# Weight loads tied to TensorE progress, one queue for the first inputs, and another block order in a fused attention and MLP layer

## The chip, the cores and the metric

The kernel runs on one core of a Trainium2 chip. The metric is the device time of one launch in microseconds, and lower is better. A core has five engines: TensorE (PE in the profile; its weight loads are listed apart as PEld), VectorE (DVE), ScalarE (ACT), GpSimd (POOL) and SyncE (SP). Transfers run on 16 DMA engines, and are issued by instructions on SP's or ACT's queue.

## The reference

One sequence of 2048 tokens of width 448 passes through an attention block and an MLP block, all in bfloat16:

```python
def _A_ref(x, wqkv, wo):               # 16 heads of 28, W, dil = 8, 2
    q, k, v = split(x @ wqkv)
    # token s attends to the tokens s, s-2, ..., s-14; those before the start are masked
    attn = softmax(einsum(q, k[idx]) * 28 ** -0.5)
    return einsum(attn, v[idx]) @ wo

def _B_ref(x, w1, w2, w3, w4):         # w1, w2: 448x448, w3: 448x1792, w4: 1792x448
    h = gelu(layernorm(x) @ w1)
    # the four quarters of h's columns are shifted by +1, -1, +2, -2 tokens
    x1 = x + shifted(h) @ w2
    return x1 + gelu(layernorm(x1) @ w3) @ w4

h = x + _A_ref(layernorm(x), wqkv, wo)
out = h + _B_ref(layernorm(h), w1, w2, w3, w4)
```

## The kernel before, in words

Tokens are handled in eight tiles m of 256 tokens each as they are loaded (two tokens to a partition). Even and odd tokens stand apart, and HT holds the transposed layer norm of 1024 even and 1024 odd tokens. A phase is a function that describes one piece of work on one tile: `phase_LN1(m)` (layer norm of the input and its transpose into HT), `phase_QK(u)` in four parts c (queries and keys), `phase_V(t)` (values), `phase_att(g)` in parts (scores, exp, sums, reciprocal by Ln and Exp, weighted values), `phase_WO(m)` and `phase_LN2(m)`, `phase_W1`, `phase_W2(m)`, `phase_LN3(m)`, `phase_W3(u)` and `phase_W4(u)` with the output's store. The layer norm runs on VectorE and GpSimd; the transposes of the first two tiles run on TensorE and the other 22 (over all three layer norms) as DMA transposes that SP issues.

Attention is made of small matmuls. A part of `phase_att` issues two groups of 64 score matmuls of 57 columns, 8 matmuls for the sums and 64 matmuls of 57 columns for the weighted values, each with its own weight load. The projections issue groups of 28 or more matmuls of 128 to 448 columns.

Nothing of the order on the engines is written by hand. The phases only make a list of operations with durations and dependencies. The planner, `_Sched.schedule` (lines 218 to 352), walks a simulated time: on each engine it takes the ready operation that can begin first, and among those that can begin within SLACK (100 ns) the one whose block stands first in the list `rank` at the end of `_fast_path`. 36 matmuls on zeros, the block "warm", have a late rank and fill TensorE where nothing else is ready. An operation waits by semaphore for each of its `deps`; its `odeps` only order it in the plan and give no wait on the chip.

The loads, with the names used below: `load_x(m)` loads two of the sixteen row groups of the input (xin). `wload` loads a 448-row weight in four pieces (two large, two small), or in eight with `each`. wqk (the query and key weights; its staging tile is called h in the profile, because it borrows the memory of h3) is needed before the first QK phase: `wqk_copies` copies it into the tile arena, which the QK matmuls read. wv are the value weights. `loads_w` (wo, w1, w2), `loads_c` (w3) and `loads_d` (w4) are the later weights, marked `bulk`. In the planner's time a bulk load is not issued before the queue's modelled end less LEAD; on the chip it waits for nothing, and in the plan it stands behind the sixth DMA transpose (`after=trs[5:6]`, an order and not a wait). In the profile w1 to w4 are all called w_s.

All instructions are issued by one helper line in `_plan` (L1324), so the profile's groups are told apart by their tiles.

Of the kernel before, what the change touches and what calls it, by code (L numbers as in the profile page):

```python
# [86 lines left out]
class _Sched:  # L87
# [86 lines left out]
    MODE = 90.0  # L174
    SLACK = 100.0
    SWITCH = 300.0
    LEAD = 500.0
    WINDOW = 3413.0

    def prepare(self):  # L180
        n = len(self.ops)
# [18 lines left out]
    def gated(self, ham, st, work):  # L200

        W = self.WINDOW
        t = st
        while work > 0.0:
            while (ham[0] + 1) * W <= t:
                ham[2] = ham[1] >= 0.38 * W if ham[2] else ham[1] >= 0.9 * W
                ham[0] += 1
                ham[1] = 0.0
            rate = 1.0 if ham[2] else 0.5
            step = min(work / rate, (ham[0] + 1) * W - t)  # L210
            t += step
            ham[1] += step
            work -= step * rate
            if work < 1e-6:
                break
        return t - st

    def schedule(self):
        if not hasattr(self, "children"):
# [53 lines left out]
        mode = None  # L273
        qfree = 0.0
        ham = [0, 0.0, False]
        done = 0
        while done < n:
            best = None
            for e in engs:
                cand = None  # L280
                for op in ready[e]:
                    st = max(arr[op.idx][e], free[e])
                    if op.bulk:
                        st = max(st, qfree - self.LEAD)
                    if cand is not None and st > cand[0] + self.SLACK:
                        continue
                    if op.opts and any(max(t2, free[e2]) + op.opts[e2][1] < st + op.opts[e][1] for e2, t2 in arr[op.idx].items()):
                        continue
                    if op.groups and e == "pe":
                        taken = ()  # L290
                        for g in op.groups:
                            if g not in gbank:
                                at = place(g.n, st, taken)
                                if at is None:
                                    break
                                st = max(st, at[1])
                                taken += tuple(range(at[0], at[0] + g.n))
                        else:
                            at = True
                        if at is None:  # L300
                            continue
                    if e == "act" and op.table is not None and op.table != table:
                        st = max(st, free[e] + self.TABLE) + self.SWITCH
                    if cand is None or st < cand[0] - self.SLACK or (st < cand[0] + self.SLACK and op.prio < cand[1].prio):
                        cand = (st, op)
                if cand is not None and (best is None or cand[0] < best[0]):
                    best = cand + (e,)
            if best is None:
                raise RuntimeError("no op can go: %r" % [(e, [(o.tag, o.idx) for o in ready[e]]) for e in engs])
            st, op, e = best  # L310
            for e2 in (op.opts or (op.eng,)):
                ready[e2].remove(op)
            i = op.idx
            eng_of[i] = e
            dur = op.opts[e][1] if op.opts else op.dur
            if e == "act" and op.table is not None:
                if op.table != table:
                    st -= self.SWITCH
                table = op.table
            if e == "pe":  # L320
                if op.mode != mode:
                    dur += self.MODE
                mode = op.mode
                dur = self.gated(ham, st, dur)
            op.t0 = beg[i] = st
            for g in op.groups:
                if g not in gbank:
                    b = place(g.n, st)[0]
                    gbank[g] = b
                    gleft[g] = len(g.ops)  # L330
                    g.bank = b
                    g.wait = set()
                    g.opener = op
                    for x in range(b, b + g.n):
                        g.wait |= {o for o in held_by[x] if o.eng != "pe"}
                        holder[x] = g
                        held_by[x] = []
                gleft[g] -= 1
                for x in range(gbank[g], gbank[g] + g.n):
                    held_by[x].append(op)  # L340
                    if gleft[g] == 0:
                        holder[x] = None
            if op.is_dma:
                free[e] = st + dur
                qfree = max(st + op.lat[0], qfree) + op.lat[1]
                op.t1 = qfree + op.lat[2]
            else:
                free[e] = st + dur + self.OCC[e]
                op.t1 = st + dur + self.LAT[e]
            fin[i] = op.t1  # L350
            order[e].append(op)
            self.gorder.append(op)
            done += 1
            for ch in self.children[i]:
                npend[ch.idx] -= 1
                if npend[ch.idx] == 0:
                    push(ch)
# [4 lines left out]
    def settle(self):  # L362
        for op in self.ops:
            if op.opts:
                op.eng = self.eng_of[op.idx]
                op.ins = op.opts[op.eng][0]
            for g in op.groups:
                if g.opener is op:
                    op.deps |= g.wait
        for op in self.ops:  # L370
            op.ins = [(m, {k: (v.fn(v.group.bank) if isinstance(v, _PV) else v) for k, v in kw.items()})
                      for m, kw in op.ins]
            for d in op.deps:
                d.users += 1
# [38 lines left out]
def _fast_path(nc, es, flag, A_x, A_wqkv, A_wo, B_w1, B_w2, B_w3, B_w4, out):  # L413
# [63 lines left out]
    def copy(out_ap, in_ap, n):  # L477
# [2 lines left out]
            "act": ([("activation", dict(ka, func=ACT.Copy))], 170 + n / 1.2),  # L480
            "dve": ([("tensor_copy", ka)], (150 + n) / 0.96)}, **ka)

    def dma(chan, out_ap, in_ap, nbytes, dur=450.0, rate=200.0, q="sp", after=(), bulk=False):
        return S.macro(q, [("dma_start", dict(out=out_ap, in_=in_ap))], dur, chan=chan, lat=(1000.0, nbytes / rate, 1150.0),
                       after=after, bulk=bulk)

    def tile(n=1):
        g = _Group(n)
# [16 lines left out]
    def wload(chan, dst, src, qs, after=(), bulk=False, each=False):  # L505
        n = src.shape[1]
        for o in range(2):
            rows = src[64 * o:64 * o + 384, :].rearrange("(i p) n -> p i n", p=128)
            for i in range(3 if each else 1):
                i0, i1 = (i, i + 1) if each else (0, 3)  # L510
                dma(chan + qs[o], dst[:, 2 * i0 + o:2 * i1 + o - 1:2, :], rows[:, i0:i1, :], 128 * n * 2 * (i1 - i0), 600,
                    rate=333.0, q=qs[o], after=after, bulk=bulk)
        for a in range(2):
            dma(chan + qs[a], dst[half[a], 6, :], src[384:448, :] if a == 0 else src[0:64, :], 64 * n * 2, 500, rate=200.0, q=qs[a],
                after=after, bulk=bulk)
# [11 lines left out]
    def setup():  # L527
        S.tag = "setup"
        load_x(0)
        load_x(1, "act")  # L530
        wload("wqk", wst, A_wqkv[:, 0:2 * D], ("sp", "act"))
        load_x(2)
        load_x(3)
        pool("memset", 150, ap=ident[:], constant=0.0)
# [51 lines left out]
    def loads_w():  # L586
        S.tag = "loads_w"
        wov = A_wo.rearrange("(c j d) n -> j d c n", c=4, j=4)
        for j in range(4):
            dma("wo%d" % j, wo_s[32 * j:32 * j + 28, :, :], wov[j], D * D * 2 // 4, 600, rate=150.0, after=trs[5:6], bulk=True)  # L590
        wload("w1", w1_s[:, 0:KB * D].rearrange("p (b n) -> p b n", b=KB), B_w1, ("sp", "sp"), after=trs[5:6], bulk=True)
        dma("w2", w2_s[:], B_w2.rearrange("(c k) n -> k c n", k=112), D * D * 2, 620, rate=300.0, after=trs[5:6], bulk=True)

    def loads_c():
        S.tag = "loads_c"
        wload("w3", w3_s, B_w3, ("sp", "sp"), after=trs[5:6], bulk=True, each=True)

    def loads_d():
        S.tag = "loads_d"
        for f in range(2):  # L600
            dma("w4_%d" % f, w4_s[:, 7 * f:7 * f + 7, :], B_w4[896 * f:896 * f + 896, :].rearrange("(f k) n -> k f n", k=128), D * F,
                740, rate=333.0, after=trs[5:6], bulk=True)

    stc = [0]

# [241 lines left out]
    def w2_ln3(*ms):  # L847
# [55 lines left out]
    phase_W3(3)  # L903
    phase_W4(3)
    rank = {b: k for k, b in enumerate((
# [6 lines left out]
    ).split())}  # L912
    for op in S.ops:
        op.prio = 10000 * rank[op.tag] + op.idx
# [483 lines left out]
```

## Time and profile before

| what | value |
|---|---|
| times of three runs | 214.65, 214.72, 215.84 us; median 214.72 us |
| the profiled execution | 214.2 us, of which its span is 212.5 us |
| TensorE busy | 191.6 us, 90% of the span, 3391 matmuls and as many weight loads |
| VectorE, ScalarE, GpSimd busy | 111.5, 100.4, 48.3 us |
| DMA | 18.13 MB, mean 85 GB/s; the first quarter of the span holds most of it |
| first QK matmul, last matmul of the MLP | 12.22 us, 206.8 us |

The page has a strip of 40 slices of the span, in which each digit is a busy share in tenths. The chain of waits follows the work that ended last backwards: a stretch called "issue" is time in which the engine waited for nothing that the profile shows. A view by windows gives each engine's busy time and number of instructions in a stretch.

### The profile page before, as it was taken

To read this page: it belongs to the slowest core of one execution; us is meant where nothing else is said; L and a number is where in the kernel's file an instruction comes from. 1 tells how busy PE (TensorE), PEld (TensorE's weight loads), DVE (VectorE), ACT (ScalarE), POOL (GpSimd) and SP (SyncE) were. 2 spreads that over 40 slices of the span, in tenths; PEclk is the share of its full clock that TensorE was granted. 3 is DMA by queue.
4 is the path that set the end of the run, shared out by engine and by line. 5 is a ranking of instruction groups with operands and counts; after the bars stand their busy time and mean duration, and the time that the engine had idled before them with its cause. 6 is when DMAs were issued, how large, how long until landed. Compare 5 with 4: busy or idle time off the path is not lost.

```text
span 212.5 us, 7395 instructions
## 1 busy us (share of the span) xinstructions
PE 191.6 (90%) x3391; PEld 129.2 (61%) x3391; DVE 111.5 (52%) x259; ACT 100.4 (47%) x107; POOL 48.3 (23%) x90
## 2 busy tenths in 40 slices
PE   7899998438899989889999999999999999999990
PEld 2367754216667678554977555888555888855540
DVE  5699635403449870989997796100998000012220
ACT  2196696506766898790965100576000566610000
POOL 6333200000003420009435049000079400000000
PEclk9999999856999999999999999999999999999999
DMA  6994799994000430004064105500015500001111
GB/s 221 321 271 88 110 202 278 283 412 112 6 5 0 93 46 3 3 6 88 3 91 58 32 4 129 86 3 3 0 26 117 119 3 3 3 0 43 43 43 54
DMA packets 29532, 18.13 MB, mean 85 GB/s; under 512 B 21112, under 2 KB 28600, under 8 KB 29496
## 3 DMA queue, kind: packets, MB, share of 16 engines
q1 hardware_dynamic: 28872, 16.58, 32.9%
q10 hardware_dynamic: 624, 1.03, 1.5%
q8 instruction: 27, 0.44, 0.8%
q14 instruction: 9, 0.07, 0.1%
HBM read 10.67 MB, written 1.84 MB: 59 GB/s over the span
## 4 chain that ended last, share of the span: by engine, by line
PE 77%; issue 6%; DMA 6%; DVE 5%; POOL 2%; ACT 2%; ACTq 0%
PE ps L1324 77%; DMA h<-in_A_wqkv_dram 4%; DVE xin L1324 2%; DMA HT<-ln 2%; POOL rstd L1324 1%; DVE QK L1324 1%; ACT lnz L1324 1%; DVE ln L1324 1%; DVE xb L1324 0%; DVE st L1324 0%; ACTq L1324 0%; ACT arena L1324 0%; ACT HT L1324 0%; POOL vtmp L1324 0%; DVE pt L1324 0%
## 5 line engine op out<-in xcount | busy, mean ns | idle before, releaser
L1324 PE MATMUL ps<-HT,w_s 64*128 64x256 bf16 (+1 forms) x1064 | 56.3, 264 | 0.8 <-DMA HT<-ln 0.6
L1324 PEld LDWEIGHTS ps<-HT,w_s 64*128 64x128 bf16 x1064 | 49.9, 94 | 7.1 <-DMA HT<-ln 0.9
L1324 DVE TENSOR_TENSOR xb<-ps,xb 128x448 bf16<-128x448 f32 (+1 forms) x24 | 18.4, 772 | 54.2 <-PE ps L1324 54.1
L1324 ACT ACTIVATE QK<-ps 128x1024 bf16<-128x1024 f32 (+2 forms) x24 | 22.7, 951 | 25.9 <-PE ps L1324 25.8
L1324 POOL TENSOR_SCALAR vtmp<-mv 128x2 f32<-128x2 f32 x32 | 6.2, 193 | 114.3 <-DVE mv L1324 112.8
L1324 PE MATMUL ps<-HT,arena 64*128 64x256 bf16 x448 | 27.5, 277 | 0.5 <-ACT HT L1324 0.5
L1324 ACT ACTIVATE arena<-ps 128x1024 bf16<-128x1024 f32 x14 | 14.3, 1024 | 24.3 <-PE ps L1324 24.3
L1324 PEld LDWEIGHTS ps<-HT,arena 64*128 64x128 bf16 x448 | 21.8, 97 | 5.8 <-ACT HT L1324 0.9
L1324 POOL TENSOR_TENSOR rstd<-vtmp,mhalf 128x2 f32<-128x2 f32 x32 | 22.3, 695 | 2.7
L1324 PE MATMUL ps<-w_s,arena 128*128 128x448 bf16 x112 | 21.5, 353 | 0.0
L1324 PE MATMUL ps<-w_s,h 128*128 128x448 bf16 x112 | 21.5, 352 | 0.0
L1324 PE MATMUL ps<-wv_s,HT 64*64 64x448 bf16 x252 | 14.8, 367 | 5.5 <-issue 5.5
L1324 DVE TENSOR_TENSOR pt<-pt,msk 128x912 bf16<-128x912 bf16 x18 | 11.2, 628 | 15.2 <-ACT pt L1324 15.2
L1324 DVE BATCH_NORM_STATS2 st<-xin 128x6 f32<-128x448 bf16 x32 | 18.3, 610 | 1.1 <-DMA xin<-in_A_x_dram 1.1
L1324 PEld LDWEIGHTS ps<-w_s,h 128*128 128x128 bf16 x112 | 11.0, 98 | 10.2
L1324 ACT ACTIVATE pt<-ps 128x912 bf16<-128x912 f32 x18 | 15.9, 930 | 2.7 <-PE ps L1324 2.7
L1324 PEld LDWEIGHTS ps<-w_s,arena 128*128 128x128 bf16 x112 | 10.9, 98 | 10.3 <-issue 0.2
L1324 ACT ACTIVATE h<-ps 128x1024 bf16<-128x1024 f32 x14 | 14.2, 1024 | 5.8 <-PE ps L1324 5.7
L1324 POOL TENSOR_TENSOR xb<-xb,xin 128x448 bf16<-128x448 bf16 x16 | 16.5, 1059 | 1.1 <-DVE ln L1324 1.0
L1324 DVE TENSOR_SCALAR ln<-xin,mv,rstd 128x448 bf16<-128x448 bf16 x32 | 14.5, 495 | 2.7 <-POOL rstd L1324 2.5
L1324 DVE TENSOR_TENSOR QK<-ps,lnz 128x456 bf16<-128x456 f32 (+1 forms) x24 | 10.9, 509 | 8.1 <-PE ps L1324 4.3
L1324 PEld LDWEIGHTS ps<-wv_s,HT 64*64 64x64 bf16 x252 | 7.1, 110 | 11.1 <-issue 7.1
(54 smaller groups left out, 171.1 us busy)
## 6 DMA issues: line engine op xcount, KB each, us to landing
w_s<-in_B_w_dram SPq DMA_DIRECT2D x6, 448.0 KB, 8.2
out_dram<-xb SPq DMA_DIRECT2D x8, 224.0 KB, 2.0
xin<-in_A_x_dram SPq DMA_DIRECT2D x7, 224.0 KB, 8.2
w_s<-in_B_w_dram SPq DMA_DIRECT2D x2, 784.0 KB, 5.8
h<-in_A_wqkv_dram ACTq DMA_DIRECT2D x1, 672.0 KB, 7.8
h<-in_A_wqkv_dram SPq DMA_DIRECT2D x1, 672.0 KB, 6.2
wv_s<-in_A_wqkv_dram SPq DMA_DIRECT2D x2, 336.0 KB, 8.5
w_s<-in_B_w_dram SPq DMA_DIRECT2D x2, 336.0 KB
```

Of the source, the lines that this page charges most:

```text
L1324: inst = getattr(eng, meth)(**kw)
```

## The change

Five edits. First, the planner knows of instruction fetches: `fetched` counts TensorE's instructions (two for each matmul), and at the 186th and after every 256 more it lets the simulated engine stand until a fetch that began at the last such boundary is over, 2900 ns plus a share of the queue's backlog. Second, every bulk load gets a dependency on a TensorE operation, the last one that in the plan ended more than 100 ns before the load; on the chip SP waits for its semaphore. The bulk loads also follow each other in the order of the program (`last`), may begin behind the first DMA transpose instead of the sixth, and LEAD is 600 instead of 500; w4 is loaded in seven pieces instead of two. Third, `load_x(1)` and the second half of wqk move from ACT's queue to SP's, so that SP issues all loads. Fourth, some durations of loads in the planner are altered. Fifth, the list `rank` is another one. No computing operation is added, removed or changed.

```diff
-    LEAD = 500.0
+    LEAD = 600.0
     WINDOW = 3413.0
+    FETCH0 = 186
+    FETCH = 2900.0
...
+    def fetched(self, fe, n, st, dur, qfree):
+
+        stall = 0.0
+        while fe[0] + n > fe[1]:
+            at = st + stall + dur * (fe[1] - fe[0]) / n
+            if at < fe[2]:
+                stall += fe[2] - at
+                at = fe[2]
+            fe[2] = at + self.FETCH + min(3600.0, 0.7 * max(0.0, qfree - at))
+            fe[1] += 256
+        fe[0] += n
+        return stall
...
         ham = [0, 0.0, False]
+        fe = [0, self.FETCH0, 0.0]
...
                 dur = self.gated(ham, st, dur)
+                dur += self.fetched(fe, 2 * len(op.ins), st, dur, qfree)
...
+        done = []
+        for op in self.gorder:
+            if op.bulk:
+                past = [d for d in done if d.t1 < op.t0 - 100.0]
+                if past:
+                    op.deps.add(max(past, key=lambda d: d.t1))
+            elif op.eng == "pe":
+                done.append(op)
...
+    last = []
+
     def dma(chan, out_ap, in_ap, nbytes, dur=450.0, rate=200.0, q="sp", after=(), bulk=False):
-        return S.macro(q, [("dma_start", dict(out=out_ap, in_=in_ap))], dur, chan=chan, lat=(1000.0, nbytes / rate, 1150.0),
-                       after=after, bulk=bulk)
+        op = S.macro(q, [("dma_start", dict(out=out_ap, in_=in_ap))], dur, chan=chan, lat=(1200.0, nbytes / rate, 1150.0),
+                     after=tuple(after) + tuple(last) if bulk else after, bulk=bulk)
+        if bulk:
+            last[:] = [op]
+        return op
...
-                dma(chan + qs[o], dst[:, 2 * i0 + o:2 * i1 + o - 1:2, :], rows[:, i0:i1, :], 128 * n * 2 * (i1 - i0), 600,
-                    rate=333.0, q=qs[o], after=after, bulk=bulk)
+                dma(chan + qs[o], dst[:, 2 * i0 + o:2 * i1 + o - 1:2, :], rows[:, i0:i1, :], 128 * n * 2 * (i1 - i0), 500,
+                    rate=320.0, q=qs[o], after=after, bulk=bulk)
...
-        load_x(1, "act")
-        wload("wqk", wst, A_wqkv[:, 0:2 * D], ("sp", "act"))
+        load_x(1)
+        wload("wqk", wst, A_wqkv[:, 0:2 * D], ("sp", "sp"))
...
-        wload("w3", w3_s, B_w3, ("sp", "sp"), after=trs[5:6], bulk=True, each=True)
+        wload("w3", w3_s, B_w3, ("sp", "sp"), after=trs[0:1], bulk=True, each=True)
...
-        for f in range(2):
-            dma("w4_%d" % f, w4_s[:, 7 * f:7 * f + 7, :], B_w4[896 * f:896 * f + 896, :].rearrange("(f k) n -> k f n", k=128), D * F,
-                740, rate=333.0, after=trs[5:6], bulk=True)
+        for f in range(7):
+            dma("w4_%d" % f, w4_s[:, 2 * f:2 * f + 2, :], B_w4[256 * f:256 * f + 256, :].rearrange("(f k) n -> k f n", k=128), 256 * 2 * D,
+                600, rate=333.0, after=trs[0:1], bulk=True)
...
     rank = {b: k for k, b in enumerate((
-        "V_3 QK_1_1 att_1_2 QK_1_0 W1_3 W3_3 att_0_1 W3_2 QK_1_2 att_0_0 W2_0 W3_0 V_2 WO_7 QK_1_3 loads_d "
...
+        "QK_1_1 QK_0_2 att_0_1 W1_5 setup QK_0_1 W2_1 WO_3 LN3_2 LN2_1 W1_0 LN3_6 LN3_7 W3_2 W4_3 LN1_2 WO_6 "
...
```

`loads_w` goes from `trs[5:6]` to `trs[0:1]` in the same way.

More of the change, by code (lines that the diff above doesn't have):

```diff
@@ L589, in loads_w @@
         for j in range(4):
-            dma("wo%d" % j, wo_s[32 * j:32 * j + 28, :, :], wov[j], D * D * 2 // 4, 600, rate=150.0, after=trs[5:6], bulk=True)
-        wload("w1", w1_s[:, 0:KB * D].rearrange("p (b n) -> p b n", b=KB), B_w1, ("sp", "sp"), after=trs[5:6], bulk=True)
-        dma("w2", w2_s[:], B_w2.rearrange("(c k) n -> k c n", k=112), D * D * 2, 620, rate=300.0, after=trs[5:6], bulk=True)
+            dma("wo%d" % j, wo_s[32 * j:32 * j + 28, :, :], wov[j], D * D * 2 // 4, 600, rate=150.0, after=trs[0:1], bulk=True)
+        wload("w1", w1_s[:, 0:KB * D].rearrange("p (b n) -> p b n", b=KB), B_w1, ("sp", "sp"), after=trs[0:1], bulk=True)
+        dma("w2", w2_s[:], B_w2.rearrange("(c k) n -> k c n", k=112), D * D * 2, 620, rate=300.0, after=trs[0:1], bulk=True)
     def loads_c():
         S.tag = "loads_c"
-        wload("w3", w3_s, B_w3, ("sp", "sp"), after=trs[5:6], bulk=True, each=True)
+        wload("w3", w3_s, B_w3, ("sp", "sp"), after=trs[0:1], bulk=True, each=True)
     def loads_d():
         S.tag = "loads_d"
-        for f in range(2):
-            dma("w4_%d" % f, w4_s[:, 7 * f:7 * f + 7, :], B_w4[896 * f:896 * f + 896, :].rearrange("(f k) n -> k f n", k=128), D * F,
-                740, rate=333.0, after=trs[5:6], bulk=True)
+        for f in range(7):
+            dma("w4_%d" % f, w4_s[:, 2 * f:2 * f + 2, :], B_w4[256 * f:256 * f + 256, :].rearrange("(f k) n -> k f n", k=128), 256 * 2 * D,
+                600, rate=333.0, after=trs[0:1], bulk=True)
     stc = [0]
```

10 rows, old and new, of the table rank are left out of this document.

## The prediction

> **What bounds the kernel now.** The page comes first, and of it the busy time by engine, the strip of slices and the list of DMA queues.
>
> ```profile
> span 212.5 us, 7395 instructions
> PE 191.6 (90%) x3391; PEld 129.2 (61%) x3391; DVE 111.5 (52%) x259; ACT 100.4 (47%) x107; POOL 48.3 (23%) x90
> PEclk9999999856999999999999999999999999999999
> DMA  6994799994000430004064105500015500001111
> q8 instruction: 27, 0.44, 0.8%
> ```
>
> TensorE is busy for 90% and no other engine for more than 52%, so time is won only where TensorE stands or runs slowly. The strip shows one such place: in slices 8 and 9 (from 42.5 us) the granted clock falls to 0.5 and 0.6, while the DMA engines are full. The chain of waits says what TensorE does there.
>
> ```profile
> 1.73 8.69 DMA h<-in_A_wqkv_dram
> ...
> 32.00 0.69 issue
> ...
> 36.84 2.05 issue
> ...
> 41.11 4.79 issue
> ...
> 52.07 0.80 issue
> ...
> 55.55 0.76 issue
> ...
> 74.99 0.91 issue
> ...
> 89.47 0.68 issue
> ```
>
> TensorE stands for nothing that the profile names. One more such stop is in the timeline of TensorE at 92.85 us (its row is below, with 0.76 us). The view by windows over the stretches between the stops tells what they are. Its columns: length; busy us (and instructions) of PE, PEld, DVE, ACT, POOL; granted clock; DMA share; GB/s.
>
> ```profile
> 22.00:26.40 4.40, 4.40 (x136) 3.43 (x128) 2.72 (x8) 2.78 (x4) 0.92 (x3) 1.00 0.85 129
> 26.40:32.00 5.60, 5.60 (x134) 2.90 (x122) 1.90 (x3) 5.25 (x7) 0.00 (x0) 1.00 1.11 195
> 32.69:36.84 4.15, 4.15 (x128) 2.62 (x128) 2.11 (x4) 2.19 (x3) 0.00 (x0) 1.00 1.12 298
> 38.89:41.11 2.22, 2.22 (x128) 1.40 (x128) 1.17 (x2) 0.89 (x2) 0.00 (x0) 1.00 1.13 269
> 45.91:52.07 6.16, 6.16 (x127) 3.70 (x127) 0.94 (x2) 2.56 (x3) 0.00 (x0) 0.56 0.68 223
> 52.86:55.55 2.69, 2.69 (x128) 1.70 (x128) 1.83 (x4) 1.82 (x3) 0.00 (x0) 1.00 0.02 6
> 90.15:92.85 2.70, 2.70 (x128) 1.76 (x128) 2.03 (x5) 2.20 (x3) 0.00 (x0) 1.00 0.02 6
> ```
>
> Between two stops there are 128 matmuls and 128 weight loads each time, whatever they are: 256 instructions. The page lists 27 instruction transfers of 0.44 MB together, 16 KB each, and TensorE's 2 x 3391 instructions make 26.5 blocks of 256. So the stops are instruction fetches: TensorE has used up a block and the next has not landed. If a fetch is asked for when TensorE enters the block before, its length is from that entry to the end of the stop. Without load it is 56.31 - 52.86 = 3.45 us, and from 90.15 to the row at 93.61 again 3.46 us. With DMA shares of 1.1 it is 32.69 - 26.40 = 6.3, 38.89 - 32.69 = 6.2, 45.90 - 38.89 = 7.0, and 52.87 - 45.91 = 7.0 us where weights covered the first two thirds. From 22.00 to 26.40 (share 0.85, DMA transposes and a first weight piece) no stop followed, so a fetch took at most 4.4 us there. [...]
>
> **The change part by part.** *Pieces behind TensorE's progress.* It removes no byte. It puts a wait before each of 24 weight loads (4 wo, 4 w1, 1 w2, 8 w3, 7 w4; 19 before), so that few pieces stand in the queue at a time, and lets them begin behind the first transpose.
>
> ```profile
> 15.40 8.64 SPq L1324 DMA_TRANSPOSE HT<-ln  x4
> 24.09 0.59 SPq L1324 DMA_DIRECT2D w_s<-in_B_w_dram  x1
> 39.73 1.12 SPq L1324 DMA_DIRECT2D w_s<-in_B_w_dram  x2
> ```
>
> Weights were issued from 24.1 to 40.9 us, and now can be from 15.4 on, where the order leaves TensorE's long matmuls. A fetch beside paced pieces has no row of its own. Its bounds are 3.45 us (no load) and 6.3 us (full queue); I take 4.4, the stretch at a share of 0.85 being the nearest row. With the blocks' own lengths (5.60, 4.15, 2.22, the fourth below, 2.69 us) the stops become 0, 0.25 and 2.18 us; the fourth block, 6.16 less 2.5 us (below) at full clock, covers a fetch of 3.45, as the weights are through by then (their share of 0.68 in its window puts their end near 50 us, and 24.1 - 15.4 = 8.7 us come off that); the fifth, already without load, stays at 0.76. Together 3.2 instead of 9.09 us: **5.9 saved**. With 3.45 throughout, only 1.23 and 0.76 are left (7.1 saved); with 6.3 see the rivals.
>
> *The clock.* The slow stretch follows these stops, as the timeline of TensorE has it (start, length, group, and in brackets the idle time before).
>
> ```profile
> 33.57 1.70 PE L1324 MATMUL ps<-HT,arena 64*128 64x256 bf16 x28
> 39.72 0.70 PE L1324 MATMUL ps<-QK 28*64 28x57 bf16 x64
> 45.91 2.07 PE L1324 MATMUL ps<-wv_s,HT 64*64 64x448 bf16 x17 [4.79 <-issue]
> 47.91 0.94 PE L1324 MATMUL ps<-QK 28*64 28x57 bf16 x64
> 48.78 2.93 PE L1324 MATMUL ps<-HT,arena 64*128 64x256 bf16 x28
> 93.61 0.62 PE L1324 MATMUL ps<-QK 28*64 28x57 bf16 x47 [0.76 <-issue]
> ```
>
> The same groups take 2.93 instead of 1.70 and 0.94 instead of 0.70 us, and the 17 value matmuls about half of 2.07 too long: 1.23 + 0.24 + 1.03 = **2.5 us**, gone if no stop is long. A remaining stop of 2.2 us after another of the kind could bring it back (the stops of 2.05 and 4.79 stood 2.2 us apart), so its lower end is nothing.
>
> *Block order.* The planner now sees a block end early and can put long matmuls between short ones. Exposed after the first edit are 2.18 + 0.76, and the three later stops 0.91, 0.68 and 0.76 with no weights near: 5.3 us. Groups of 64 short matmuls cannot be divided, two of them last 1.4 us by the 0.70 row, and exp, sums and values follow one another in a fixed chain, so I take a third, **1.8 saved**, between nothing and 5.3. The list also reorders the rest; for that no row gives a sign.
>
> *One queue at the start.* TensorE's first QK matmul, at 12.22 us, waits for copies of wqk and for the second tile's HT.
>
> ```profile
> 5.43 1.12 DVE L1324 BATCH_NORM_STATS2 st<-xin 128x6 f32<-128x448 bf16 x2
> 9.70 0.56 PE L1324 MATMUL ps<-ident,ln 128*128 128x128 bf16 x7 [0.46 <-DVE ln L1324]
> 10.50 0.86 ACT L1324 ACTIVATE arena<-h 128x784 bf16<-128x784 bf16 x1 [1.39 <-DMA h<-in_A_wqkv_dram]
> 11.27 0.90 ACT L1324 ACTIVATE HT<-ps 128x896 bf16<-128x896 bf16 x1
> ```
>
> The last of wqk lands at 10.42 us (1.73 + 8.69) by ACT's queue, while SP's queue already moves later tiles and wv beside it. On one queue all of wqk stands ahead of these. But the HT copy cannot start before 9.70 + 0.56 = 10.26, against 11.27 now: at most 1.0 us. The other way, x1 is issued behind x0, and VectorE began on it at 5.43 us without a wait; an issue later, by the 0.59 us of one SP issue, shifts the second tile by as much. Between 0.6 lost and 1.0 won I take **0.5 won**, as wqk is what the chain names. All of it counts, since TensorE then works without a gap up to 32.0 us.
>
> *What the waits hold up.* On SP's queue the six transposes of the first layer norm now stand among waiting pieces, and TensorE waits for these transposes.
>
> ```profile
> 22.63 3.23 PE L1324 MATMUL ps<-HT,arena 64*128 64x256 bf16 x56
> ...
> L1324 SPq DMA_TRANSPOSE HT<-ln x6: 1222/1320/3567, 15.4 to 26.1; - x6
> ...
> DMA to landing us min/median/max: 3.0/3.2/7.7
> ```
>
> A transpose lands after 3.2 us, behind weights after up to 7.7, 4.5 more. The second one, issued about 16.7 and landing about 19.9, is needed by QK_1 at 22.63, 2.7 us later: 0 to 1.8 us lost, I take **0.9**. Tiles 4 to 7 are needed after 30 us and have cover.
>
> Sum against the profiled execution: 214.2 - 5.9 - 2.5 - 1.8 - 0.5 + 0.9 = **204.4 us**. The three runs' median, 214.72, is 0.5 above that execution and their lowest 0.45; I add nothing for that, as it is less than the step for the transposes is unsure by. The end behind the last matmul (206.8 to 212.5, and 1.7 around the span) is untouched.
>
> **The rivals.**
>
> *Pacing does not shorten a fetch* as long as any piece is in flight. For it: all loaded fetches cost 6.2 to 7.0 us, however much still stood in the queue. Against it: the 4.4 us at a share of 0.85. Fetches of 6.3 for three blocks leave 0.7 + 2.15 + 4.08, then 0 and 0.76 without load: 7.7, only 1.4 saved, and the slow clock stays. 214.2 - 1.4 - 0.5 - 1.0 (a third of the three later stops and the 0.76) + 0.9 = **212.2 us**. [...] Chance 0.14.
>
> *The stops only move.* The new order puts short groups together elsewhere. Grouped by tile and shape (busy us, mean ns of one | idle before) there are:
>
> ```profile
> L1324 PE MATMUL ps<-pt,vt 64*32 64x57 bf16 x576 | 7.1, 192 | 5.2 <-issue 5.2
> L1324 PE MATMUL ps<-QK 28*64 28x57 bf16 x576 | 6.9, 197 | 0.8 <-issue 0.8
> ```
>
> These 1152 have to go somewhere, and at 64 in 0.70 us a block of them lasts 1.4 us against a fetch of 3.45. Stops and clock loss stay in sum, only the start is won: **213.7 us**. [...] Chance 0.08.
>
> *SP held by TensorE (slower).* A piece waits for TensorE, the transposes behind it wait for the piece, TensorE for the transposes. It takes place between 15 and 40 us with tiles 3 to 7. Each turn costs up to a landing behind a wait, 3.2 us; four turns are 12.8, and such stops leave the clock loss of 2.5 where it is: 214.2 - 5.9 - 1.8 - 0.5 + 12.8 = **218.8 us**. It decides from about 10 us of new waits, the size of the gains. For it: no wait on SP's weights existed before. Against it: the layer norm of the input needs nothing of TensorE behind its first two tiles, and TensorE has value and query work from the tiles already there. Chance 0.10.
>
> *All stops go*, late ones too, the clock stays up and the start wins 1.0: 214.2 - 11.4 - 2.5 - 1.0 = **199.3 us**. Chance 0.05. The forecast has 0.63; its own ends are 201.2 (fetches of 3.45 with 7.1 saved, two thirds of the 4.3 us of stops then left, no transpose loss: 214.2 - 7.1 - 2.5 - 2.9 - 0.5) and 208.7 (no gain from the order and the clock loss kept: 214.2 - 5.9 - 0.5 + 0.9).
>
> **How the numbers follow.** Within 1% (212.6 to 216.9) is about what cannot be told from no change. Faster: forecast 0.63, all stops 0.05, half of the first rival at its edge 0.07: 0.75. Same: the other half 0.07 and the moved stops 0.08: 0.15. Slower: 0.10. The range from 200.5 to 212.5 takes in the forecast and most of the first rival, and leaves out about 0.2: the best case, the moved stops and SP held.
>
> **What would show it.** Right: between 25 and 60 us no issue stop over 2.5 us, a clock strip of nines, weights spread from about 16 us at a DMA share below 1, stops still 128 matmuls apart; the first QK matmul before 12 us. Wrong: stops of 3 us and more beside single pieces (the first rival), as many stops elsewhere (the second), or TensorE waiting for DMA HT<-ln between 15 and 40 us (the third).

## The result

The changed kernel takes 206.94 us (median of four executions, 205.88 to 209.00) against 214.69 us (213.43 to 215.84) for the kernel before, run beside it: a ratio of 0.962, with a 95% interval of 0.955 to 0.970. Forecast were 204.4 us, in a range of 200.5 to 212.5. The ratios here and below leave out executions that are more than 1.5% above the fastest of their kernel, such as the one of 209.0 us, whose profile is shown first.

The page of the changed kernel, in the same parts as before:

```profile
span 207.2 us, 7398 instructions
PE 191.5 (92%) x3391; PEld 129.7 (63%) x3391; DVE 112.2 (54%) x261; ACT 101.8 (49%) x107; POOL 48.2 (23%) x90
PEclk9999999998899999979999999999999999999999
DMA  5996596654467500050252002561000231001111
```

TensorE's busy time has not changed, as no matmul was added or removed. With the slices counted from 0, as in the prediction, the DMA engines are no longer full in slices 5 to 8; the same bytes are spread up to slice 13. There are still two weak stretches in the clock, in slices 9 and 10 (from 46.6 us) and in slice 17 (from 88.1 us). The chain of waits:

```profile
3.31 9.02 DMA h<-in_A_wqkv_dram
...
35.49 0.81 issue
...
40.15 0.29 issue
...
47.99 1.49 issue
...
86.02 1.15 issue
```

With one of 0.40 us before 83.61 us, these are all the stops of TensorE from the first QK matmul on that have no releaser and last over 0.2 us: 4.14 us instead of 11.44. The view by windows over three stretches that start where a block was entered shows again 256 instructions to a block (130 and 127 matmuls by this record):

```profile
32.70:35.49 2.79, 2.79 (x130) 1.66 (x126) 2.01 (x3) 2.70 (x4) 0.00 (x0) 1.00 0.58 158
36.31:40.15 3.84, 3.84 (x127) 2.74 (x128) 2.44 (x4) 2.35 (x4) 0.00 (x0) 1.00 0.70 209
40.44:44.20 3.76, 3.76 (x127) 3.05 (x127) 0.00 (x0) 2.67 (x4) 0.00 (x0) 1.00 0.64 236
```

The timeline of TensorE shows the start and the two places where the clock is lost:

```profile
13.19 5.07 PE L1354 MATMUL ps<-HT,arena 64*128 64x256 bf16 x84 [2.35 <-DVE arena L1354]
...
40.44 1.25 PE L1354 MATMUL ps<-HT,arena 64*128 64x256 bf16 x19 [0.29 <-issue]
...
45.52 1.70 PE L1354 MATMUL ps<-HT,arena 64*128 64x256 bf16 x28 [0.51 <-DVE QK L1354]
...
49.48 0.30 PE L1354 MATMUL ps<-pt,vt 64*32 64x57 bf16 x28 [1.49 <-issue]
49.71 6.42 PE L1354 MATMUL ps<-HT,arena 64*128 64x256 bf16 x84
...
87.17 0.34 PE L1354 MATMUL ps<-QK 28*64 28x57 bf16 x19 [1.15 <-issue]
87.44 2.83 PE L1354 MATMUL ps<-wv_s,HT 64*64 64x448 bf16 x28
90.20 6.55 PE L1354 MATMUL ps<-wo_s,QK 128*128 128x448 bf16 x32
```

The span fell by 5.3 us in these two executions, and that is accounted for. The stops give 7.3. The first QK matmul begins at 13.19 instead of 12.22 us, which takes back 1.0: TensorE waits 2.35 us for copies of wqk, which lands at 12.33 instead of 10.42 us. The clock costs 1.66 us behind 49.71 (the 84 QK matmuls take 4.76 us at full clock in a variant below) and 1.3 + 0.3 behind 87.44 (28 value matmuls take 1.52 us, the 32 WO matmuls 6.26, in the kernel before): 3.3 us, where before had lost 2.5. TensorE's other waits and short gaps grew by 0.7, and the stretch behind its last matmul is 0.45 us shorter.

SP's queue shows where the loads went (start, length of the whole group, count):

```profile
16.84 2.07 SPq L1354 DMA_TRANSPOSE HT<-ln  x1
...
29.78 34.04 SPq L1354 DMA_DIRECT2D w_s<-in_B_w_dram  x19
```

The pieces of w1 to w4 are issued between 29.8 and 63.8 us; before they were issued from 24.1 to 40.9 us.

### The profile page after: what moved, and what is told of

The parts are those of the page before. It is cut to its first block, busy times and chain, and to the rows that moved or that the text cites. A ratio compares the mean times of both kernels' runs of the same rounds, so it can differ in the third digit from the quotient of the medians.

```text
span 207.2 us, 7398 instructions
## 1 busy us (share of the span) xinstructions
PE 191.5 (92%) x3391; PEld 129.7 (63%) x3391; DVE 112.2 (54%) x261; ACT 101.8 (49%) x107; POOL 48.2 (23%) x90
## 4 chain that ended last, share of the span: by engine, by line
PE 77%; DMA 7%; DVE 6%; ACT 3%; issue 3%; SPq 1%; POOL 1%
PE ps L1354 77%; DMA h<-in_A_wqkv_dram 4%; DMA HT<-ln 2%; DVE xin L1354 1%; ACT lnz L1354 1%; ACT pt L1354 1%; DVE pt L1354 1%; SPq L1354 1%; DVE st L1354 1%; DVE xb L1354 1%; DVE ln L1354 1%; POOL rstd L1354 1%; ACT QK L1354 0%; DVE arena L1354 0%; DVE mv L1354 0%
## 5 line engine op out<-in xcount | busy, mean ns | idle before, releaser
L1354 ACT ACTIVATE arena<-ps 128x1024 bf16<-128x1024 f32 x14 | 14.3, 1024 | 36.1 <-PE ps L1354 36.1
L1354 PE MATMUL ps<-HT,arena 64*128 64x256 bf16 x448 | 28.1, 280 | 3.3 <-DVE arena L1354 2.3
L1354 ACT ACTIVATE QK<-ps 128x1024 bf16<-128x1024 f32 (+2 forms) x23 | 21.6, 948 | 14.2 <-PE ps L1354 14.1
L1354 PEld LDWEIGHTS ps<-HT,arena 64*128 64x128 bf16 x448 | 22.5, 98 | 8.6 <-issue 4.6
L1354 ACT ACTIVATE h<-ps 128x1024 bf16<-128x1024 f32 x14 | 14.3, 1024 | 12.5 <-PE ps L1354 12.5
L1354 PE MATMUL ps<-wv_s,HT 64*64 64x448 bf16 x252 | 14.2, 376 | 0.0
L1354 PE MATMUL ps<-wo_s,QK 128*128 128x448 bf16 x64 | 12.9, 358 | 0.0
```

The source lines that it names most:

```text
L1354: inst = getattr(eng, meth)(**kw)
```

## The experiments

Eight variants were run, and three kernels twice or more. Each ratio is against the kernel before on the same chip. Executions of one kernel on one chip differ by up to 2.7% (211.67 to 217.47 us for the kernel before), so the ratios near 1 are only as good as their intervals.

**The changed kernel again.** Run twice more, to see whether the late start is its own.

> The changed kernel once more, for a profile beside the others. Expected: 205.5 to 207.5 us. If the late start (first QK matmul at 13.2 us, wqk landing at 12.3 us) belongs to the change, it is there again within 0.5 us; if it was that one execution, the first QK matmul is back near 12.2 us.

> The changed kernel on the same chip as the variants: 206 to 208 us, first QK matmul at 13.0 to 13.5 us.

Medians of 207.89 us (206.06 to 210.43; ratio 0.969, 0.960 to 0.978) and 207.99 us (206.09 to 209.74; 0.968, 0.960 to 0.976). The first median lies above the 205.5 to 207.5 us expected. The first QK matmul came at 13.40 us in the first of the two profiles and at 12.36 in the second, below what was expected of it; wqk landed at 12.54 and 11.51 us. So the landing varies by a microsecond, and in all three profiles is later than the 10.42 us of before.

The second of these profiles, the third of this kernel (208.45 us), has the long stops of the first and another clock:

```profile
44.40 1.70 PE L1354 MATMUL ps<-HT,arena 64*128 64x256 bf16 x28 [0.50 <-DVE QK L1354]
...
48.37 0.30 PE L1354 MATMUL ps<-pt,vt 64*32 64x57 bf16 x28 [1.49 <-issue]
48.60 4.76 PE L1354 MATMUL ps<-HT,arena 64*128 64x256 bf16 x84
...
85.52 2.83 PE L1354 MATMUL ps<-wv_s,HT 64*64 64x448 bf16 x28
88.28 7.70 PE L1354 MATMUL ps<-wo_s,QK 128*128 128x448 bf16 x32
```

TensorE stands for 0.50 and 1.49 us, as it did for 0.51 and 1.49, but the 84 QK matmuls behind take 4.76 us instead of 6.42: nothing is lost. So the length of these stops does not decide on the clock by itself. The late loss is there again, and larger: 2.7 us over the 1.52 and 6.26 us of the kernel before, whose row for the 28 value matmuls is:

```profile
91.06 1.52 PE L1324 MATMUL ps<-wv_s,HT 64*64 64x448 bf16 x28
```

In all eight profiles with the new order (this kernel, and the variants of it below, with the waits and without) these 28 matmuls take 2.83 us; in the four profiles with the order of before in which no stop divides them they take 1.52. This loss, 1.4 to 2.8 us with the 32 WO matmuls that follow, thus comes with the new order. From the first QK matmul to the last matmul, in the trace of the kernel before and in the first one of the changed kernel, the granted clock is 1.00 or 0.50: 0.50 for 10.24 us on end in the kernel before (41.10 to 51.34 us), and for 3.41 us at each of two places in the changed kernel (from 49.94 and from 87.49 us).

**Waits taken away.** The order on every engine stays, only SP's waits for TensorE go:

```diff
-        done = []
-        for op in self.gorder:
-            if op.bulk:
...
-            elif op.eng == "pe":
-                done.append(op)
```

> The changed kernel with the same order on every engine, but the later weight loads wait for nothing on TensorE. Theory (pacing): the queue fills from about 19 us on, fetches between 28 and 50 us cost 6 to 7 us again, the stops there sum to 7 to 11 us instead of 2.6, and the time is 211 to 214 us. [...] Rival (the block order did it): within 1 us of the changed kernel.

213.39 us (211.09 to 216.02; ratio 0.992, 0.986 to 0.998), 5.5 us above the 207.89 of the changed kernel on the same chip. SP's queue and TensorE's stops:

```profile
28.93 14.34 SPq L1346 DMA_DIRECT2D w_s<-in_B_w_dram  x19
```

```profile
35.57 0.28 PE L1346 MATMUL ps<-pt,vt 64*32 64x57 bf16 x23 [0.80 <-issue]
...
41.63 1.25 PE L1346 MATMUL ps<-HT,arena 64*128 64x256 bf16 x19 [2.21 <-issue]
...
49.39 0.78 PE L1346 MATMUL ps<-QK 28*64 28x57 bf16 x56 [2.51 <-issue]
```

The same 19 loads are issued in 14.3 us instead of 34.0, and the stop of 0.29 us becomes 2.21. One of 2.51 us stands a block later, where the first profile of the changed kernel has none, and its stop of 1.49 us, another block on, is gone. From the end of one stop to the end of the next, which is one fetch if it is asked for when a block is entered, as the prediction has it, it is 41.63 - 35.57 = 6.06 and 49.39 - 41.63 = 7.76 us. The stops ahead of 60 us sum to 5.5, less than the 7 to 11 expected, as blocks in the new order are longer, but the time is in the range that the theory of pacing gave. The rival that the block order did it, which put the time within 1 us of the changed kernel, is refuted.

**Two queues at the start.** After planning, three loads are given back to ACT; all else keeps its order:

```diff
     order = S.schedule()
+    moved = [op for op in order["sp"] if op.chan in ("x1", "wqkact") and prefix == "f_"]
+    order["sp"] = [op for op in order["sp"] if op not in moved]
+    order["act"] = moved + order["act"]
...
```

> The changed kernel with x1 and one large and one small piece of wqk issued by ACT again, all else in the same order. Theory (one queue makes wqk land late): wqk lands at about 10.5 us, the first QK matmul begins by 12.3 us, and the time is 1 to 2 us below the changed kernel, 204.5 to 205.5 us. Rival (the landing differs from execution to execution, or bytes ahead of it set it): no change that can be told, 206 to 207 us.

> The variant with two queues at the start once more: first QK matmul at 11.5 to 12 us again, 205.8 to 206.5 us, slow clock only near 85 us.

206.09 us (205.81 to 206.44; ratio 0.963, 0.956 to 0.971), beside 207.89 for the changed kernel on the same chip. The difference is the 1 to 2 us expected, but the time lies above the 204.5 to 205.5 us of the theory and in the range of the rival. The second run gave 207.29, above the range given for it. TensorE in the first run:

```profile
11.62 5.07 PE L1362 MATMUL ps<-HT,arena 64*128 64x256 bf16 x84
...
34.76 0.28 PE L1362 MATMUL ps<-pt,vt 64*32 64x57 bf16 x23 [0.83 <-issue]
...
39.17 1.25 PE L1362 MATMUL ps<-HT,arena 64*128 64x256 bf16 x19 [0.57 <-issue]
...
43.93 0.63 PE L1362 MATMUL ps<-QK 28*64 28x57 bf16 x56 [0.83 <-issue]
...
47.93 0.30 PE L1362 MATMUL ps<-pt,vt 64*32 64x57 bf16 x28 [0.39 <-issue]
48.17 4.76 PE L1362 MATMUL ps<-HT,arena 64*128 64x256 bf16 x84
```

QK begins at 11.62 us (11.42 in the second run), 0.7 to 2.0 us ahead of the changed kernel's three profiles. The intervals of the times overlap, so the gain in time is likely and not shown. A fetch beside paced pieces, from the end of one stop to the end of the next, took 39.17 - 34.76 = 4.41, then 4.76 and 4.00 us here; the kernel with waits alone, below, has a wider range. No clock is lost at 48.17 us behind a stop of 0.39 us.

**One queue alone.** The same edit the other way on the kernel before: ACT's three loads go to SP.

> The kernel before with ACT's three loads moved to SP, in the order x0, x1, the two large and the two small pieces of wqk; all else as before. Theory (one queue makes wqk land later): wqk lands 1 to 2 us later than the 10.4 us of before, the first QK matmul begins at 12.8 to 13.5 us, and the time is 0.5 to 1.5 us above the kernel before, 214.5 to 216.5 us. Rival (bytes ahead of it set the landing, as the prediction had it): wqk lands before 10 us and the first QK matmul begins before 12 us.

216.29 us (215.63 to 217.02) against 214.23, a ratio of 1.014 (1.006 to 1.023). The kernel before took from 211.67 to 217.47 us on that chip, so that the edit alone makes it slower is likely and not clear.

```profile
11.23 0.86 ACT L1335 ACTIVATE arena<-h 128x784 bf16<-128x784 bf16 x1 [2.33 <-DMA h<-in_A_wqkv_dram]
...
12.95 6.38 PE L1335 MATMUL ps<-HT,arena 64*128 64x256 bf16 x112 [1.39 <-ACT HT L1335]
```

The copies of wqk start at 11.23 us (10.50 before), 0.7 later, somewhat less than the 1 to 2 us expected, and QK at 12.95 (12.22 before). The stops ahead of 60 us are also 1.0 us longer in this profile (10.1 instead of 9.1), so not all of the time is the start. In the whole set the last of wqk landed at 10.7 to 12.5 us with one queue (six profiles, mean 11.6) and at 10.1 to 11.5 with two (eight profiles, seven of them below 10.9, mean 10.5): about a microsecond, in ranges that overlap. With one queue its last piece is issued at 3.3 us instead of 1.7, behind five others at 0.4 to 0.55 us each, and it then takes 7.4 to 9.2 us to land in the six profiles, against 8.69 in the kernel before. Why its own time hardly shrinks although its bytes stand ahead of the others was not settled.

**Waits alone.** The kernel before with its own order, and only the loop above added:

> The kernel before, same order on every engine, with only the waits for TensorE added ahead of its 19 later weight loads. Theory (pacing): the stops between 32 and 57 us fall from 9.1 to about 3 to 4 us, and the time is 206 to 209 us, the lower end if the slow clock goes too. Rival (depth of the queue does not matter): the weights are in flight for longer and as many blocks wait, 213 to 217 us. Rival (the block order did it): 213 to 215 us.

> The kernel before with waits alone, once more, for a second profile. Its earlier times went from 207.6 to 211.4 us, and the profiled one, 207.6 us, had no slow clock. If the clock makes the spread, an execution near 210 us shows slices below 9 in the strip of the clock and the same stops within 0.5 us each.

210.30 us (207.62 to 211.37; ratio 0.986, 0.978 to 0.993), and 209.46 in the second run. The first:

```profile
32.74 0.94 PE L1332 MATMUL ps<-wv_s,HT 64*64 64x448 bf16 x14 [1.17 <-issue]
...
37.84 0.58 PE L1332 MATMUL ps<-pt,vt 64*32 64x57 bf16 x52 [0.95 <-issue]
...
41.30 1.13 PE L1332 MATMUL ps<-wv_s,HT 64*64 64x448 bf16 x17 [1.23 <-issue]
...
48.95 0.29 PE L1332 MATMUL ps<-pt,vt 64*32 64x57 bf16 x26 [1.29 <-issue]
```

The stop of 4.79 us is now 1.23, and the stops ahead of 60 us are 4.9 instead of 9.1 (3 to 4 were expected). A fetch, taken in the same way, was 37.84 - 32.74 = 5.10 and 41.30 - 37.84 = 3.46 us here. The median lies above the 206 to 209 us expected. The second run says why:

```profile
PEclk9999999759999999999999999999999999999998
```

```profile
32.91 0.94 PE L1332 MATMUL ps<-wv_s,HT 64*64 64x448 bf16 x14 [0.67 <-issue]
...
38.83 0.58 PE L1332 MATMUL ps<-pt,vt 64*32 64x57 bf16 x52 [1.77 <-issue]
...
42.56 2.07 PE L1332 MATMUL ps<-wv_s,HT 64*64 64x448 bf16 x17 [0.48 <-issue]
```

Here one stop was 1.77 us, the clock fell behind it, and the 17 value matmuls took 2.07 instead of 1.13 us, though this execution's stops ahead of 60 us are smaller in sum (4.0). The slow clock costs some 2.3 us in five groups behind that stop (0.24, 0.57, 0.94, 0.23 and 0.34 us), more than the 1.8 us between the two executions. A stop of 1.58 us at 71.83 us cost no clock in this execution, and one of 1.56 us at 69.45 none in the first. The fetches were 38.83 - 32.91 = 5.92 and 42.56 - 38.83 = 3.73 us. The stops themselves were not the same within 0.5 us, as that expectation had them.

**Order alone.** The changed kernel with two queues at the start and without the waits, so with the new order, the new places of the loads and w4 in seven pieces:

> The changed kernel without the waits and with two queues at the start, so that against the kernel before only the order of the work and the place of the loads in it differ. Theory (the parts add up): 1 to 1.5 us below the one without waits, 211.5 to 212.5 us, that is 2 to 3 us gained by the order with stops of about 8 us; waits alone gained 4.5 us. Rival (the order gains only together with the waits): 213.5 to 215 us.

212.06 us (209.34 to 214.28; ratio 0.992, 0.985 to 0.998). So waits alone give about 1.4%, the order alone 0.8%, and both together (two queues) 3.7%. By these ratios order and waits do more together than their sum, though their intervals are some 0.7% wide to either side. One queue costs 1.4% in the kernel before and nothing that can be told in the changed kernel without waits: 0.992 with one queue and 0.992 with two, where the first QK matmul begins at 12.46 and at 12.31 us.

**The list of blocks of before, under the new planner.** Only `rank` is put back.

> The changed kernel with the list of blocks of the kernel before; the planner still counts fetches and the waits are there. Theory (most of the gain is the waits, the order a smaller part): 207.5 to 210.5 us, near the kernel before with waits alone, with 6 to 8 us of stops. Rival (the order matters as much as the waits): above 211 us. Rival (the order does nothing): 206 to 207.5 us.

238.80 us (237.67 to 239.60; ratio 1.117, 1.110 to 1.125), outside all that was expected. The stops are not the cause, as they sum to 5.6 us; TensorE waits longer for the transposes of the layer norms:

```profile
145.18 16.19 PE L1354 MATMUL ps<-HT,w_s 64*128 64x256 bf16 x280 [4.94 <-DMA HT<-ln]
...
187.43 23.16 PE L1354 MATMUL ps<-HT,w_s 64*128 64x256 bf16 x392 [6.39 <-DMA HT<-ln]
```

In that plan the layer norms come too late for W3, late in the kernel where no weight is loaded. The list only breaks ties in one planner's simulated time; with other durations in it the same list gives another order, and a bad one. So this run does not measure the order.

**Blocks moved.** In the kernel before, fillers are split so that 32 more matmuls stand ahead of all real work.

```diff
-            pe([mm(T(lambda p: p[:, 0, 0:512]), flat[:, 0:128], flat[:, 128:640], True, True)], 216, "full")
+            n, c = (5, 64) if k < 8 else (1, 128 if k < 13 else 512)
+            pe([mm(T(lambda p, c=c: p[:, 0, 0:c]), flat[:, 0:128], flat[:, 128:128 + c], True, True)] * n, 216, "full")
```

> The kernel before; of its first 13 fillers on zeros, eight are five narrow matmuls each and five are narrower ones, so that 32 matmuls (64 instructions) more stand ahead of all real work. Theory (stops are fetches of blocks of 256 instructions): every stop comes 32 matmuls earlier in the program: the first no longer splits the 28 value matmuls 14 to 14 but falls into the 64 score matmuls ahead of them, the long one no longer splits value matmuls 11 to 17 but falls into the 64 score matmuls ahead, and stops still stand 128 matmuls apart. Rival (the stops belong to what TensorE does there): they stay where they are in the order of work.

214.84 us in its one execution. TensorE at the two long stops:

```profile
30.85 0.66 PE L1325 MATMUL ps<-QK 28*64 28x57 bf16 x59
33.66 0.22 PE L1325 MATMUL ps<-QK 28*64 28x57 bf16 x5 [2.14 <-issue]
...
42.36 0.53 PE L1325 MATMUL ps<-QK 28*64 28x57 bf16 x43
47.24 0.53 PE L1325 MATMUL ps<-QK 28*64 28x57 bf16 x21 [4.35 <-issue]
```

The two stops split 64 score matmuls at 59 and at 43. From the old places (14 into the value matmuls, with 13 matmuls between them and the scores; 11 into the value matmuls right behind the scores) 32 back are 5 and 21 from the end of the scores: exactly these. In this kernel a stop belongs to a count of instructions and not to what TensorE does there.

**Weights where TensorE has long matmuls.** The variant with two queues, with w1 to w3 issued from 44 us and w4 from 85 us in the profile, by new begin times after planning:

```diff
+    late = [op for op in order["sp"] if op.bulk and op.chan[:2] != "wo"]
+    begin = (44000, 45200, 46400, 46700, 47200, 48600, 50100, 51600, 53100, 54600, 56100, 57600, 58400,
+             81000, 82500, 84000, 85500, 87000, 88500, 90000)
...
```

> The variant with two queues at the start, all compute engines in the same order, but w1, w2 and w3 are issued only where TensorE has long matmuls (from about 48 us), w4 from about 85 us; wo stays. Theory (a fetch costs 3.45 us alone and about a microsecond more beside a paced piece): the stops between 33 and 48 us fall from 2.6 us to below 1, none arises between 48 and 74 us, and the time is 203.5 to 205 us. Rival (a fetch beside pieces costs no more than one alone): no change, 205.8 to 206.4 us. Rival (the later transposes now wait behind pieces): TensorE waits for HT between 60 and 75 us or 95 and 105 us, above 206.5 us.

206.07 us (205.08 to 207.55; ratio 0.967, 0.961 to 0.972): above the 203.5 to 205 us expected, and no better than two queues alone (206.09, 0.963).

```profile
44.31 12.14 SPq L1371 DMA_DIRECT2D w_s<-in_B_w_dram  x11
```

```profile
44.95 0.30 PE L1371 MATMUL ps<-pt,vt 64*32 64x57 bf16 x28 [0.40 <-issue]
...
85.20 7.47 PE L1371 MATMUL ps<-wo_s,QK 128*128 128x448 bf16 x32
```

The stops ahead of 60 us fell from 2.6 to 0.40 us, as the theory had it, so a fetch beside a paced piece (4.00 to 4.76 us with two queues, above) cost more here than one alone (3.45 us in the kernel before). The profiled execution took 205.1 us, but the median did not follow. In this profile the 32 WO matmuls take 7.47 us instead of 6.34 in the first run with two queues; in the second run they took 7.64. All these profiles lose clock behind the late stops of 1.15 to 1.27 us that end between 82.0 and 84.7 us; whether that alone hides the gain is open. The later transposes do not: TensorE waits 0.60 us for HT at 66.71 us, and 0.50 us at that place with two queues alone.

No version was found that is clearly faster than the changed kernel.

## Why the prediction was right, point by point

**The stops are fetches of 256 instructions:** right. The moved blocks show that a stop goes by the count of instructions; that it is a fetch rests on the 27 instruction transfers of 16 KB and on the stops' growth with the loads beside them. One of these transfers moved within the stop of 4.79 us of the kernel before.

**Pieces behind TensorE's progress, 5.9 us:** right in size, and the main part. The fetch beside paced pieces was taken at 4.4 us between bounds of 3.45 and 6.3; from the end of one stop to the end of the next it measured 4.0 to 4.8 with two queues and 3.5 to 5.9 in the two runs with waits alone, so 4.4 is a fair middle and not a constant. Stops ahead of 60 us went from 9.1 to 2.3 to 2.6 us in three profiles, 6.5 to 6.8 saved with the order's share in it. Without the waits, 5.5 us of time come back (213.39 against 207.89). One step under it was wrong: the weights were to move ahead by 8.7 us, being free from 15.4 us on, and to be through by the fourth block. In fact only wo was issued that early, the others from 29.8 to 63.8 us, spread by the waits. The fourth and fifth blocks therefore still had pieces beside them.

**The clock, 2.5 us saved:** wrong, nothing was saved. The step put it as "gone if no stop is long", with a lower end of nothing. No stop is long now, and the clock still falls. The first profile loses 1.7 us at 49 us, behind 0.51 and 1.49 us of standing, and 1.6 us behind 0.63 and 1.15 us at 87; the second loses 1.7 us at 39 us, behind 1.41 us, and again the late part; the third loses nothing ahead of 60 us, with the stops of the first, and 2.7 us at the second place. What the prediction did not see is that the new order brings a loss at that second place, the 28 value matmuls and what follows them, where the kernel before has none. Why the clock falls behind some stops and not behind others of the same length stays open. Without its 2.5 us the forecast would have been 206.9 us; that this is the median measured is luck, as the start was missed too.

**Block order, 1.8 us:** not separable as written. With the term before it, it left 3.7 us of stops in all; measured were 4.1 to 4.5 in three profiles. Late stops (behind 60 us) went only from 2.35 to between 1.55 and 2.2 us, so little of the third is there. But the order alone gains 0.8%, and more with the waits, in spite of the late loss of clock. One premise was wrong: a part of `phase_att` issues its scores in two groups of 32 matmuls and not of 64, so scores can be divided; only the 64 matmuls for the values are one group.

**One queue, 0.5 us won:** the sign was wrong. QK begins 0.1 to 1.2 us later than before in the three profiles of the changed kernel, and in time the edit costs between nothing and 1.4%, by the pairs above. The step that failed is that all of wqk stands ahead of later loads and so lands sooner. The price that was left out is SP's time to issue six pieces one behind the other, 1.6 us for the last. In the first profile of the changed kernel this issue time is on the chain of work that ended last, where the last piece of wqk is issued at 3.31 us.

**What the waits hold up, 0.9 us lost:** not seen. The first layer norm's six transposes landed after 3.2 us as before, the slowest after 4.5 instead of 7.7:

```profile
DMA to landing us min/median/max: 2.9/3.2/4.5
```

TensorE waited for none of them. The value was the middle of 0 and 1.8; it measured 0. Only the four wo pieces, of 98 KB each, stand among these transposes; that their size is the reason was not tested.

**The rivals.** That pacing does not shorten a fetch is refuted by the kernel without waits. From the end of one stop to the end of the next it was 3.5 to 5.9 us beside paced pieces, and 6.1 to 7.8 us beside a full queue in the kernel before and in the one without waits. Whether the number of waiting pieces makes the difference or the bytes moved at the time was not told apart: the DMA share was 0.58 to 0.70 in the blocks of the changed kernel shown above, 1.11 to 1.13 in the kernel before, and 1.02 to 1.06 in three stretches of the kernel without waits between 32.7 and 44.2 us. That stops only move, and that SP is held by TensorE, did not happen.

**The signs.** Of what was to show that the forecast is right, the longest stop (1.49 us, none over 2.5 between 25 and 60 us) and the 128 matmuls from stop to stop are there. The clock strip of nines and the first QK matmul before 12 us are not, and w1 to w4 begin at 29.8 and not at 16 us.

So the sign and the main term were right; two smaller terms failed together. Against the first profile, 4.6 us above the forecast, the clock misses by 3.3 us (0.8 lost instead of 2.5 saved), the start by 1.5 and the stops by 0.4; the other waits cost 0.2 us less than the transposes were given, and the end behind the last matmul gave 0.45.

## What to carry to other kernels

Where a trace shows an engine standing with no releaser, count its instructions between the stops: a constant count that moves with instructions added ahead, as here (256 from stop to stop, and both long stops 64 instructions earlier in the work behind 64 added ones), points to fetches. Here the cure was to keep bulk loads from standing deep in the queues while short instructions run, by giving a wait to loads that had tens of microseconds to spare: without the waits the changed kernel took 213.39 us, with them 207.89. Before loads are put on one queue, count the issue times ahead of the piece that ends last (five of 0.4 to 0.55 us each here); and do not book a clock gain as long as stops of about a microsecond remain close together (here the clock fell behind 0.51 and 1.49 us, and behind 0.63 and 1.15), and look for new slow stretches wherever the order of work has changed.

## What was not expected of the hardware

The granted clock fell without one long stop: behind 1.77 us in one place in the kernel with waits alone (38.8 us), and behind 0.51 and 1.49 us in the changed one. But 0.50 and 1.49 us did not do it in another execution of the changed kernel, nor did 1.56 and 1.58 us with waits alone, nor 0.83 and 0.39 us with smaller waits between (two queues, 47.9 us). Two executions of one kernel thus differed in which stops brought it about.
